# Fused attention and two expert layers: plain fp32 second tiles, halved opening transfers, and a second expert layer whose first gather precedes the search

## The chip, the cores and the metric

The kernel runs on one core of a Trainium2 chip, so nothing is exchanged with other cores. The metric is the device time of one execution in microseconds, the median of several runs. The engines are named as the profile does: PE is TensorE (PEld its weight loads), DVE VectorE, ACT ScalarE, POOL GpSimd, SP the queue engine that issues most DMAs; POOL issues the gathers and scatters by index.

## The reference, cut to what matters

```python
x = attn(q, k, v)            # 4 x 8 heads, 576 positions, head size 64, block-causal -> x: 2304 x 512
# stage 0: top-1 of 8 experts with a capacity of 576
logits = x @ w_gate; e = argmax(logits); gate = softmax(logits)[e]
keep = rank of the token among those of its expert < capacity
out = gate * (relu(x @ w1[e]) @ w2[e]) if keep else 0
# stage 1: on the result, for tokens with x @ w_skip > 0, without a capacity
y = gate2 * (relu(x @ w1b[e2]) @ w2b[e2])
out = x + y                  # the other tokens pass through
```

w1 is 512 x 1024 and w2 1024 x 512 for each expert, all fp32.

## The kernel before, in words

Attention runs over 32 heads. Its loop executes the table TURN once per head, and a hook after each entry issues side work: weights of stage 0's first expert into the eight tiles raw[0], zeros into the output (both through load_more, one 512 KB transfer per head), and steps of the routing generators.

A stage then works through tiles of 128 tokens, grouped by expert. The rows of a tile are gathered from X in HBM into XN by an indirect DMA of POOL, transposed on PE, and copied by ACT: as plain fp32 into x32, or as a high and a low part into xt. There are two ways to multiply. raw_products takes the fp32 weights as they landed (ph is the first layer, 32 products of 128 columns; py the second, 8 of 512 columns; the trace has two records for each fp32 product). products takes weights that were split into a high part (ACT) and a low part (a subtraction on DVE or POOL) in W, needs x and h split and transposed as well, and uses 24 + 24 products of 512 columns. A first tile of an expert can be raw while the weights are split beside it.

After a tile, prev scales py into Yx, scatters it to the output by the indices pidx and, in stage 0, routes those rows for stage 1 (transposes, logits, pick) and scatters Yx to X. put then enters the picked rows into the second router's table. Each is a generator whose steps are placed between the matmuls.

first(s, ...) opens a stage. Its order is written by hand in the strings of AHEAD: entry n + 1 lists what follows group n of the 24 groups of matmuls of the tile. S is one of the 16 half-tile splits, C a step of the chain (in the first tile of stage 0 the last routing of attention's output; of stage 1 the last put and prev of stage 0; in the second tile the table that orders the experts, and the gather of the third tile), A a step of prev, G the search for the first rows and the second expert with its gather, K the copy of XN and the gather of the second tile's rows, X and Y the transposes of the next rows, L a load of the second expert's weights, T the turn-over (pidx, XP). Tile one is written by at, tile two by at2 (inside a branch taken when the first expert has two full tiles, as it has here). Later tiles come from body. lo names the engine of each split's subtraction.

Engines run in order, each through its own queue; a value that steers a branch or a DMA is loaded into every engine's registers (TENSOR_LOAD) at the head of each block. SP issues in order; the reload of raw[0] for later users is queued there.

## Time and profile before

| | |
|---|---|
| median of 3 runs | 796.57 us (796.44 to 803.91) |
| the profiled execution | 797.4 us, of which the span is 795.5 us |
| mean granted clock of PE | 0.959 |
| busy: PE, DVE, ACT, POOL | 695.7, 444.3, 365.6, 322.1 us |
| attention | 0 to 247.8 us |
| stage 0, first tile at | 247.8 us; second 273.2; third 289.7 |
| stage 1, first tile at | 562.2 us; second 578.8; third 594.0 |

The span runs from the first to the last instruction; a stage begins where its first product does. Busy time of PE is modelled and overlaps at the edges, so starts of successive groups say more than durations.

### The profile page before, as it was taken

How to read it: one execution, taken by the hardware profiler on the slowest of the kernel's cores; microseconds unless marked ns; L12 is line 12 of the kernel's file. 1: busy time of each engine (PE TensorE's matmuls, PEld its weight loads, DVE VectorE, ACT ScalarE, POOL GpSimd, SP SyncE). 2: the span in 40 equal slices, each digit the busy share in tenths (PEclk: the TensorE clock that was granted, in tenths of full speed). 3: DMA queues.
4: the chain of work that ended last, by engine and by line, in shares of the span. 5: the costliest groups of instructions: out<-in, count | busy, mean ns of one | idle time of the engine just before them, and what ended most of it. 6: DMA issues, size and time to landing. Idle time of an engine off the chain costs nothing. (4 is left out here: it accounts for less than half of the span.)

```text
span 795.5 us, 14329 instructions
## 1 busy us (share of the span) xinstructions
PE 695.7 (87%) x4288; PEld 522.6 (66%) x4288; DVE 444.3 (56%) x1389; ACT 365.6 (46%) x886; POOL 322.1 (40%) x362
## 2 busy tenths in 40 slices
PE   5999989989988769987899999994889989999991
PEld 4878767768766447765567776672667667777860
DVE  5877897798875623421263435443532767632473
ACT  4877656757755123311353324432412565522371
POOL 5766555556505412211242223322533446341362
PEclk9999999999999789998999999997799999999996
DMA  8799959849312675425771111111639488110000
GB/s 169 149 220 205 227 143 194 209 81 152 69 46 57 225 260 172 134 74 194 248 258 42 60 44 44 42 64 58 222 130 367 146 282 298 37 54 16 32 25 14
DMA packets 107000, 108.61 MB, mean 137 GB/s; under 512 B 66599, under 2 KB 75815, under 8 KB 106832
## 3 DMA queue, kind: packets, MB, share of 16 engines
q1 hardware_dynamic: 100192, 87.62, 41.0%
q0 software_dynamic: 6640, 19.07, 7.2%
q8 instruction: 67, 1.10, 0.6%
q14 instruction: 101, 0.83, 0.3%
HBM read 102.81 MB, written 22.30 MB: 157 GB/s over the span
## 5 line engine op out<-in xcount | busy, mean ns | idle before, releaser
L867 PE MATMUL ph<-W,xt 128*128 128x512 f32 x456 | 127.3, 417 | 2.2 <-ACTq L1149 0.8
L843 PE MATMUL ph<-x,raw 128*128 128x128 f32 x832 | 105.6, 286 | 21.5 <-issue 9.0
L876 PE MATMUL py<-W,hT 128*128 128x512 f32 x456 | 120.4, 403 | 1.5 <-DVE hT L738 1.5
L843 PEld LDWEIGHTS ph<-x,raw 128*128 128x128 f32 x832 | 100.8, 200 | 29.9 <-issue 12.7
L714 DVE TENSOR_TENSOR W<-raw,W 128x512 fp32r<-128x512 f32 x107 | 100.4, 974 | 22.6 <-ACT W L712 19.6
L867 PEld LDWEIGHTS ph<-W,xt 128*128 128x128 f32 x456 | 81.8, 191 | 24.5 <-issue 5.5
L850 PE MATMUL py<-raw,h 128*128 128x512 f32 x208 | 96.7, 606 | 0.0
L712 ACT CAST W<-raw 128x512 fp32r<-128x512 f32 x160 | 87.6, 617 | 15.3 <-DVE full L963 6.5
L876 PEld LDWEIGHTS py<-W,hT 128*128 128x128 f32 x456 | 82.0, 189 | 18.9 <-DVE hT L738 2.2
L206 ACT ACTIVATE P<-s,nm 128x576 f32<-128x576 f32 (+4 forms) x160 | 82.7, 524 | 18.1 <-DVE nm L199 13.9
L719 POOL DMA_INDIRECT XN<-X,nidx x30 | 33.8, 1126 | 140.0 <-DVE ohv1b L503 75.2
L714 POOL TENSOR_TENSOR W<-raw,W 128x512 fp32r<-128x512 f32 x53 | 71.6, 1362 | 40.5 <-ACT W L712 40.1
L199 DVE TENSOR_REDUCE nm<-s 128x1 f32<-128x576 f32 (+4 forms) x160 | 75.3, 487 | 4.5 <-DVE s L197 0.2
L31 PE MATMUL pt<-ident,P 128*128 128x128 f32 x480 | 74.4, 283 | 1.6 <-DVE xr L1253 0.9
L187 PE MATMUL s<-KT,QT 128*128 128x320 f32 (+1 forms) x192 | 64.5, 348 | 4.9 <-ACT P L206 4.8
L106 ACT COPY PT<-pt 128x448 f32<-128x448 f32 (+2 forms) x96 | 47.2, 492 | 41.4 <-PE pt L31 41.2
L738 DVE TENSOR_TENSOR hT<-t,hT 128x512 fp32r<-128x512 f32 x38 | 26.3, 692 | 69.4 <-ACT hT L737 69.2
L31 PEld LDWEIGHTS pt<-ident,P 128*128 128x128 f32 x480 | 51.9, 142 | 17.7 <-DVE s L197 5.5
L890 ACT ACTIVATE h<-ph 128x512 f32<-128x512 f32 x38 | 22.7, 598 | 86.1 <-PE ph L867 86.1
L850 PEld LDWEIGHTS py<-raw,h 128*128 128x128 f32 x208 | 37.8, 195 | 36.1 <-issue 36.1
L188 PE MATMUL s<-KS,QT 128*128 128x320 f32 (+1 forms) x192 | 55.7, 314 | 4.6 <-DMA KS<-KT 4.6
L262 PE MATMUL o<-PT,vs 128*64 128x256 f32 (+3 forms) x448 | 56.4, 368 | 0.5 <-ACT xT L106 0.5
(256 smaller groups left out, 1037.5 us busy)
## 6 DMA issues: line engine op xcount, KB each, us to landing
raw<-in_moe_w_dram SPq DMA_DIRECT2D x152, 512.0 KB
KS<-KT SPq DMA_DIRECT2D x64, 144.0 KB
ks<-in_k_dram SPq DMA_DIRECT2D x32, 144.0 KB
qs<-in_q_dram SPq DMA_DIRECT2D x32, 144.0 KB
out_dram<-XN SPq DMA_DIRECT2D x9, 512.0 KB
vs<-in_v_dram SPq DMA_DIRECT2D x32, 128.0 KB
X<-xr SPq DMA_DIRECT2D x16, 256.0 KB
v<-in_v_dram SPq DMA_DIRECT2D x16, 32.0 KB
```

Source lines behind the costliest of these rows:

```text
L31: nc.tensor.transpose(out, in_, ident)
L187: nc.tensor.matmul(out=out, lhsT=lhs, rhs=kT[:, a:e], start=True, stop=False)
L188: nc.tensor.matmul(out=out, lhsT=lhs, rhs=kS[:, a:e].bitcast(F32R), start=False, stop=True)
L199: self.nc.vector.reduce_max(out=nm[:m], in_=self.sv[h, i], axis=AX.X, negate=True)
L206: self.nc.scalar.activation(P[:m, PO[i]:PO[i] + KN[i]], self.sv.pop((h, i)), AF.Exp, bias=self.nm.pop((h, i))[:m], accum_out=sm[:m, i:i + 1],)
L262: nc.tensor.matmul(out=ps[64 * j:64 * j + 64, a - q0:q1 - q0], lhsT=vs[:, j, c, :] if c < 4 else self.v4[p % 3][:, j], rhs=PT[:, KO[c] + a ...
L712: nc.scalar.copy(hi, src)
L714: eng.tensor_tensor(out=lo, in0=src, in1=hi.bitcast(F32), op=ALU.subtract)
L843: nc.tensor.matmul(out=ph[j // 4][:, 128 * (j % 4):128 * (j % 4) + 128], lhsT=raw[c][:, 128 * j:128 * j + 128], rhs=self.x32[:, 128 * c:12 ...
L850: nc.tensor.matmul(out=self.py, lhsT=self.h32[c // 4][:, 128 * (c % 4):128 * (c % 4) + 128], rhs=raw[4 + c // 2][:, 512 * (c % 2):512 * (c ...
L867: nc.tensor.matmul(out=ps, lhsT=xt[p][:, 128 * c:128 * c + 128], rhs=W[w][c][:, 512 * half:512 * half + 512], start=n == 0, stop=n == 11,)
L876: nc.tensor.matmul(out=ps, lhsT=self.hT[c // 4][p][:, 128 * (c % 4):128 * (c % 4) + 128], rhs=W[w][4 + c // 2][:, 512 * (c % 2):512 * (c % ...
```

## The change

The second tile of each stage is computed by raw_products, so its rows are only copied to x32, and the weights need to be split by the third tile. All 16 subtractions go to DVE; six (stage 0) or eight (stage 1) splits lie in the first tile and the rest in the second. The first tile's result has buffers of its own, Y0 and pidx0. raw[0] is reloaded after the second tile. In stage 1, G stops at the gather, the search for the second expert (H) comes behind the products of the first layer, and most steps of the chain come after the first products. In stage 0 the routing chain is no longer interleaved with splits. In attention, the weights and zeros go out in transfers of 256 KB, up to two per head, over heads 9 to 29 in place of one of 512 KB per head over heads 4 to 20. h serves both kinds of tile (h32 is gone).

```diff
-    def prev(self, s):
-        nc = self.nc
+    def prev(self, s, first=False):
+        nc = self.nc
+        Yx, pidx = (self.Y0, self.pidx0) if first else (self.Yx, self.pidx)
         gate = self.XP[:, DM:DM + 1]
         if s == 0:
-            nc.scalar.activation(self.Yx[:, 0:DM], self.py, AF.Copy, scale=gate)
+            nc.scalar.activation(Yx[:, 0:DM], self.py, AF.Copy, scale=gate)
         else:
             nc.vector.scalar_tensor_tensor(
-                out=self.Yx[:, 0:DM], in0=self.py, scalar=gate, in1=self.XP[:, 0:DM], op0=ALU.mult, op1=ALU.add
+                out=Yx[:, 0:DM], in0=self.py, scalar=gate, in1=self.XP[:, 0:DM], op0=ALU.mult, op1=ALU.add
             )
         yield
-        self.indirect(self.out, self.Yx[:, 0:DM], self.pidx, scatter=True)
+        self.indirect(self.out, Yx[:, 0:DM], pidx, scatter=True)
         if s:
             return
-        ps = self.t4(self.Yx)
+        ps = self.t4(Yx)
         nc.scalar.copy(self.yT, ps)
         yield
...
         yield from self.r2.pick(
-            self.lg, self.valid, self.pval, self.Yx[:, DM:DM + 1],
-            lambda: self.indirect(self.X, self.Yx, self.pidx, scatter=True),
+            self.lg, self.valid, self.pval, Yx[:, DM:DM + 1],
+            lambda: self.indirect(self.X, Yx, pidx, scatter=True),
         )
...
-                        out=self.py, lhsT=self.h32[c // 4][:, 128 * (c % 4):128 * (c % 4) + 128],
+                        out=self.py, lhsT=self.h[c // 4][:, 128 * (c % 4):128 * (c % 4) + 128],
                         rhs=raw[4 + c // 2][:, 512 * (c % 2):512 * (c % 2) + 512], start=c == 0, stop=c == 7,
                     )
             if n in (5, 11):
-                nc.scalar.activation(self.h32[n // 6], ph[n // 6], AF.Relu)
+                nc.scalar.activation(self.h[n // 6], ph[n // 6], AF.Relu)
             at(n)
...
     def first(self, s, router, chain, after=None, cap=None):
         nc, tc = self.nc, self.tc
         plan = self.AHEAD[s]
+
         split = self.split(s, self.raw[0], plan["lo"])
+        done = plan["at"].count("S")
+        ahead = self.ahead(s, router)
...
-            self.reload(s, 0, range(8))
+            if not two:
+                self.reload(s, 0, range(8))
             router.index(self.idx[s], router.T, "i")
...
             elif t == "G":
-                for _ in self.ahead(s, router):
+                for _ in range(3):
+                    next(ahead)
+            elif t == "H":
+                for _ in ahead:
                     pass
             elif t == "Y":
                 self.next_x("r")
             elif t == "X":
-                self.next_x("x")
+                self.next_x("r")
...
             elif t == "K":
                 self.keep(s, self.XC, self.XN)
                 self.gather(s, self.XN, self.pre[:, 1:2], self.rows)
             elif t == "T":
-                self.turn_over(s, lambda: nc.vector.tensor_copy(self.pidx, self.pre[:, 0:1]))
-
-        script(plan["at"], one, True)
-        for x in split, chain, load:
+                self.turn_over(s, self.pidx0, lambda: nc.vector.tensor_copy(self.pidx0, self.pre[:, 0:1]))
+
+        script(plan["at"], one)
+        for x in chain, load:
...
         with tc.If(flag(2) > 0) as two:
-            steps, prev = experts(True), self.prev(s)
+            steps, prev, rest = experts(True), self.prev(s, True), self.split(s, self.raw[0], plan["lo"], done)
 
             def act(t):
                 if t == "A":
                     next(prev, None)
+                elif t == "S":
+                    next(rest, None)
...
@@ -1076,13 +1086,19 @@
                 elif t == "T":
                     for _ in prev:
                         pass
-                    self.turn_over(s, lambda: nc.vector.tensor_copy(self.pidx, self.pre[:, 1:2]))
+                    self.turn_over(s, self.pidx, lambda: nc.vector.tensor_copy(self.pidx, self.pre[:, 1:2]))
 
             script(plan["at2"], act)
+            for _ in rest:
+                pass
+            self.reload(s, 0, range(8))
         with two.Else():
+            for _ in self.split(s, self.raw[0], plan["lo"], done):
+                pass
             for _ in experts(False):
                 pass
             self.next_x("xr")
+            nc.vector.tensor_copy(self.pidx, self.pidx0)
         self.count = {k: self.value(0, k) for k in range(2)}
         self.base, self.number = {0: 0}, {}
         self.base[1] = self.value(3, 1, mybir.EngineType.DVE)
@@ -1090,14 +1106,14 @@
 
     AHEAD = (
         dict(
-            lo="VPPVPPVPPPPPPPVV",
-            at="KSSSCCCCCCCCCC SS S S S CCSCC CSSC S S S S S S CCC CC CC C CLLL LLL LL C C CX C CT",
-            at2="KCCCCC C CC - AAA CAC CA AAC A CC - - - - AAAC - - A - - X - - - T",
+            lo="VVVVVVVVVVVVVVVV",
+            at="KCCCCCCCCCC - - - - CCCC CCCCCCCC CCC - S - S S S - S - LLLS LLL LLC - - X - T",
+            at2="KACCCCC CC CA C CA C CA CAS AS AS AS AS S S S S S - - X - - - - T",
         ),
         dict(
-            lo="PVPVVPVPPPPVVPPP",
-            at="GSCCCCCSSCSCCSCSCYKCCCCS SSC CSC - - SS - CCCCS LCCS CSLCC L LCL C LSLL - - X - - C - - - - T",
-            at2="KAACCCCCCCC - C C - - - CCCCC - - - - - - - - - - - - X - - - T",
+            lo="VVVVVVVVVVVVVVVV",
+            at="GCCCCYK CC CC - C CC C CCCCCCC H - - - CL CL LLS LLS LLS S S S S X S - T",
+            at2="KACCCCC CCA C C CS CS CS S S S S S S - - - - - - X - - - - T",
         ),
     )
...
+        def weights(i):
+            m, h = i // 2, i % 2
+            t, w1, w2 = raw[0][m][:, 512 * h:512 * h + 512], w11, w12
+            if m < 4:
+                nc.sync.dma_start(out=t, in_=w1[0, 128 * m:128 * m + 128, 512 * h:512 * h + 512])
+            else:
+                r = 256 * (m - 4) + 128 * h
+                nc.sync.dma_start(out=t, in_=w2[0, r:r + 128, :])
+
+        def zeros(i):
+            nc.sync.dma_start(out=out[128 * i:128 * i + 128, :], in_=M.XN[:, 0:DM])
+
+        def capacity_value():
+            nc.vector.tensor_copy(capf[:, 0:1], capi[:, 0:1].bitcast(U32))
...
+        def load_more(h, part):
+            n = 2 * h + part
+            if n == 6:
                 load_small()
-            elif step < 8:
-                m = step
-                w1, w2 = w11, w12
-                t = raw[0][m]
...
+            i = n - 18
+            if 0 <= i < 42 and i % 5 != 4:
+                i -= i // 5
+                if i % 2 == 0 and i < 32:
+                    weights(i // 2)
                 else:
...
+                    zeros(i // 2 if i < 32 else i - 16)
 
...
@@ -1335,8 +1357,8 @@
         step, n = [0], len(A.TURN)
 
         def hook():
-            if step[0] % n == 0:
-                load_more(step[0] // n - 10)
+            if step[0] % n in (0, n // 2):
+                load_more(step[0] // n - 6, int(step[0] % n > 0))
             if step[0] % n in A.SIDE:
```

Three places show how the order moves. DVE in the first tile of stage 0, from the rank to the first ORa (rra and ranka are ranks, OJa and ORa the operands of the permute matmuls that TensorE waits for, W the low parts), before:

```order
L429 TENSOR_REDUCE ranka<-rra 128x5
L432 TENSOR_TENSOR gea<-j_80,ranka 128x95
L714 TENSOR_TENSOR W_3844<-raw_179,W_3836 128x512 x2
L435 SCALAR_TENSOR_TENSOR kva<-ranka,cap,vb 128x5
L438 TENSOR_TENSOR Ja<-gea 128x90
L440 TENSOR_REDUCE rma<-gea 128x5
L443 TENSOR_TENSOR ohva<-oha,kva 128x40
L444 SCALAR_TENSOR_TENSOR rma<-rma,ranka 128x5
L449 TENSOR_TENSOR OJa<-ohva,Ja 128x144
L455 TENSOR_SCALAR ORa<-iotam,rma 128x128
```

and after, from the rank on:

```order
L429 TENSOR_REDUCE ranka<-rra 128x5
L432 TENSOR_TENSOR gea<-j_80,ranka 128x95
L435 SCALAR_TENSOR_TENSOR kva<-ranka,cap,vb 128x5
L438 TENSOR_TENSOR Ja<-gea 128x90
L440 TENSOR_REDUCE rma<-gea 128x5
L443 TENSOR_TENSOR ohva<-oha,kva 128x40
L444 SCALAR_TENSOR_TENSOR rma<-rma,ranka 128x5
L449 TENSOR_TENSOR OJa<-ohva,Ja 128x144
L455 TENSOR_SCALAR ORa<-iotam,rma 128x128
L449 TENSOR_TENSOR OJa<-ohva,Ja 128x144
L455 TENSOR_SCALAR ORa<-iotam,rma 128x128
```

The two subtractions between gea and kva are gone; six subtractions now stand behind the fifth ORa, ahead of the sum into Ta.

PE at the end of the first tile of stage 0 and the start of the second (pt is the permute), before:

```order
L850 MATMUL py<-raw_177,h_3863 128x512 x2
L850 MATMUL py<-raw_178,h_3864 128x512
L462 MATMUL pt<-OJa,ORa 128x144 x5
L850 MATMUL py<-raw_178,h_3864 128x512
L31 MATMUL t<-ident,XN 128x128 x4
L850 MATMUL py<-raw_179,h_3864 128x512 x2
L988 TENSOR_LOAD flags
L1062 COMPARE_AND_BRANCH
L867 MATMUL ph<-W_3829,xt_196 128x512
L867 MATMUL ph<-W_3830,xt_196 128x512
L867 MATMUL ph<-W_3831,xt_196 128x512
```

and after, with the start of the second tile and the place of the first result's transposes:

```order
L462 MATMUL pt<-OJa,ORa 128x144 x5
L854 MATMUL py<-raw_178,h_3875 128x512 x2
L31 MATMUL t<-ident,XN 128x128 x4
L854 MATMUL py<-raw_179,h_3875 128x512 x2
L995 TENSOR_LOAD flags
L1070 COMPARE_AND_BRANCH
L847 MATMUL ph<-x_198,raw_172 128x128
L847 MATMUL ph<-x_198,raw_173 128x128
L847 MATMUL ph<-x_198,raw_174 128x128
L847 MATMUL ph<-x_198,raw_175 128x128
L847 MATMUL ph<-x_198,raw_172 128x128
L31 MATMUL t<-ident,Y_3881 128x128 x4
```

The permute stands one product earlier, and the second tile begins with raw products, with the transposes of Y0 (here Y_3881) after five of them.

PE at the opening of stage 1 (oh1b, OJb and ORb belong to put, lgT to prev, XN holds the gathered rows), before:

```order
L508 MATMUL g<-oh1b,ONE 128x8
L31 MATMUL t<-ident,Yx 128x128 x4
L765 MATMUL g<-yT,w_171 32x128 x4
L31 MATMUL g<-ident,lgT 128x128
L541 MATMUL g<-OJb,ORb 128x144
L31 MATMUL t<-ident,XN 128x128 x4
L507 LDWEIGHTS LT
L507 MATMUL g<-oh1b,LT 128x16
L508 LDWEIGHTS ONE
L508 MATMUL g<-oh1b,ONE 128x8
L843 MATMUL ph<-x_198,raw_172 128x128
L843 MATMUL ph<-x_198,raw_173 128x128
```

and after:

```order
L508 MATMUL g<-oh1b,ONE 128x8
L31 MATMUL t<-ident,Yx 128x128 x4
L769 MATMUL g<-yT,w_171 32x128 x4
L31 MATMUL g<-ident,lgT 128x128
L31 MATMUL t<-ident,XN 128x128 x4
L847 MATMUL ph<-x_198,raw_172 128x128
L847 MATMUL ph<-x_198,raw_173 128x128
L847 MATMUL ph<-x_198,raw_174 128x128
```

The put matmuls on ORb and the second pair on oh1b no longer stand ahead of the first raw product.

## Rows read from the trace of the kernel before

**Rows 1.** Windows by stage (from:to, length, busy us per engine with instructions, clock, DMA share, GB/s).
```profile
247.80:311.70 63.90, 50.19 (x247) 35.74 (x246) 33.61 (x113) 19.81 (x40) 22.63 (x23) 0.87 0.57 193
...
543.00:594.80 51.80, 34.44 (x170) 25.92 (x171) 22.62 (x89) 15.73 (x30) 22.55 (x21) 0.80 0.40 139
```

**Rows 2.** Timeline of PE, first tile of stage 0 (start, us, instruction, [idle <-releaser]).
```profile
252.07 0.20 PE L408 MATMUL pt<-oha,LT 128*128 128x48 bf16 x1 [1.23 <-DVE oha L398]
...
256.56 4.46 PE L850 MATMUL py<-raw,h 128*128 128x512 f32 x10
266.08 2.06 PE L462 MATMUL pt<-OJa,ORa 128*128 128x144 f32 x5 [5.06 <-DVE ORa L455]
...
273.22 2.53 PE L867 MATMUL ph<-W,xt 128*128 128x512 f32 x8
```

**Rows 3.** Timeline of DVE in the same tile, and one row of POOL.
```profile
250.12 1.04 DVE L380 TENSOR_TENSOR eva<-lg,mxa 128x40 f32<-128x40 f32 x1
...
253.64 0.84 DVE L714 TENSOR_TENSOR W<-raw,W 128x512 fp32r<-128x512 f32 x1 [0.87 <-ACT W L712]
...
258.21 0.20 DVE L429 TENSOR_REDUCE ranka<-rra 128x5 f32<-128x40 f32 x1
...
259.40 3.48 DVE L714 TENSOR_TENSOR W<-raw,W 128x512 fp32r<-128x512 f32 x2
...
264.27 1.12 DVE L443 TENSOR_TENSOR ohva<-oha,kva 128x40 f32<-128x40 bf16 x1
...
267.31 0.28 DVE L455 TENSOR_SCALAR ORa<-iotam,rma 128x128 fp32r<-128x128 f32 x1
...
252.64 12.70 POOL L714 TENSOR_TENSOR W<-raw,W 128x512 fp32r<-128x512 f32 x9 [1.54 <-ACT W L712]
```

**Rows 4.** Timeline of all engines between the second and third tile of stage 0.
```profile
289.67 0.73 PE L867 MATMUL ph<-W,xt 128*128 128x512 f32 x2 [0.78 <-ACTq L1149]
292.41 0.15 DVE L1079 COPY pidx<-pre 128x1 int32<-128x1 int32 x1 [3.55 <-DMA X<-Yx,pidx]
...
296.13 1.08 PE L31 MATMUL t<-ident,Yx 128*128 128x128 f32 x4 [5.73 <-DVEq L1149]
```

**Rows 5.** Timeline of PE: two tiles of stage 0, then a raw tile of stage 1.
```profile
311.69 0.63 PE L867 MATMUL ph<-W,xt 128*128 128x512 f32 x2
...
326.26 0.63 PE L867 MATMUL ph<-W,xt 128*128 128x512 f32 x2
...
654.69 7.38 PE L843 MATMUL ph<-x,raw 128*128 128x128 f32 x64 [0.90 <-ACT W L712]
...
668.82 4.53 PE L867 MATMUL ph<-W,xt 128*128 128x512 f32 x16
```

**Rows 6.** Timelines of DVE, POOL and PE at the opening of stage 1.
```profile
548.08 0.21 DVE L963 TENSOR_SCALAR full<-cntb 128x1 f32<-128x1 f32 x2 [5.11 <-DVEq L1143]
...
550.21 1.07 POOL L719 DMA_INDIRECT XN<-X,pre  x1 [11.86 <-DVE actb L559]
...
553.45 0.17 PE L507 MATMUL g<-oh1b,LT 128*128 128x16 bf16 x1 [10.48 <-DVE oh1b L501]
...
560.17 0.46 PE L541 MATMUL g<-OJb,ORb 128*128 128x144 f32 x1 [3.30 <-DVE ORb L538]
...
562.22 6.54 PE L843 MATMUL ph<-x,raw 128*128 128x128 f32 x36 [0.52 <-ACT x L741]
...
578.75 4.31 PE L867 MATMUL ph<-W,xt 128*128 128x512 f32 x16
```

**Rows 7.** Timeline of PE, start of the third tile of stage 1.
```profile
594.04 1.17 PE L867 MATMUL ph<-W,xt 128*128 128x512 f32 x4 [0.70 <-PEq L1149]
```

**Rows 8.** Window of the second tile of stage 0.
```profile
273.20:289.70 16.50, 14.81 (x76) 10.79 (x74) 7.78 (x34) 4.99 (x10) 3.51 (x5) 0.99 0.40 127
```

**Rows 9.** DMA issues: the gathers by pre (count, median us to landing).
```profile
XN<-X,pre POOLq DMA_INDIRECT x4, 3.5
```

**Rows 10.** Waits of PE in attention (us in total, times, longest).
```profile
PE s L188 <- DMA KS<-KT: 4.6, 5, 1.7
```

More of the change, by code (lines that the diff above doesn't have):

```diff
@@ L650, in open @@
         self.hT = [[st.tile([128, 512], F32R, name=f"hT{i}{p}") for p in range(2)] for i in range(2)]
-        self.h32 = [st.tile([128, 512], F32, name=f"h32{i}") for i in range(2)]
         self.Yx = st.tile([128, DM + 1], F32, name="Yx")
+        self.Y0 = st.tile([128, DM + 1], F32, name="Y0")
+        self.pidx0 = st.tile([128, 1], I32, name="pidx0")
         self.yT = st.tile([128, DM], F32, name="yT")
@@ L660, in open @@
         nc.gpsimd.memset(self.Yx, 0.0)
+        nc.gpsimd.memset(self.Y0, 0.0)
     def more(self):
@@ L700, with split @@
     )
-    def split(self, s, raw, lows=None):
+    def split(self, s, raw, lows=None, start=0):
         nc = self.nc
         lows = lows or self.PLAN[s]["lo"]
-        for n, i in enumerate(self.ORDER):
+        for n, i in list(enumerate(self.ORDER))[start:]:
             k, o = i // 2, 512 * (i % 2)
@@ L822, in keep, with turn_over @@
         )
-    def turn_over(self, s, rows):
+    def turn_over(self, s, pidx, rows):
         nc = self.nc
@@ L829, in turn_over @@
         if s == 0:
-            nc.vector.tensor_scalar_add(self.pval, self.pidx, 1.0)
+            nc.vector.tensor_scalar_add(self.pval, pidx, 1.0)
             nc.vector.tensor_scalar(
@@ L913, in at @@
                         pass
-                self.turn_over(s, lambda: self.column(self.idx[s], self.pidx, self.base[k] + j))
+                self.turn_over(s, self.pidx, lambda: self.column(self.idx[s], self.pidx, self.base[k] + j))
             if n == turn[2]:
@@ L1015, in experts, with script @@
             self.later, self.number = self.value(0, 3, sp), {3: self.value(4, 3, sp)}
-            self.reload(s, 0, range(8))
+            if not two:
+                self.reload(s, 0, range(8))
             router.index(self.idx[s], router.T, "i")
             yield
-        def script(text, act, raw=False):
+        def script(text, act):
             text = text.split()
@@ L1027, in at @@
                     act(t)
-            if raw:
-                self.raw_products(self.raw[0], at)
-            else:
-                self.products(s, at)
+            self.raw_products(self.raw[0], at)
         load = loads()
@@ L1211, in load_small @@
             nc.sync.dma_start(out=w9[:, :, NE], in_=wskip.rearrange("(c p) -> p c", p=128))
-        def load_more(step):
-            if step < -1:
-                return
-            if step == -1:
-                load_small()
-            elif step < 8:
-                m = step
-                w1, w2 = w11, w12
-                t = raw[0][m]
-                if m < 4:
-                    nc.sync.dma_start(out=t, in_=w1[0, 128 * m:128 * m + 128, :])
-                else:
-                    nc.sync.dma_start(
-                        out=t.rearrange("p (c d) -> p c d", c=2),
-                        in_=w2[0, 256 * (m - 4):256 * (m - 4) + 256, :].rearrange("(c p) d -> p c d", p=128),
-                    )
-            elif step < 17:
-                m, n = step - 8, NTOK // 9
-                nc.sync.dma_start(
-                    out=out[n * m:n * m + n, :].rearrange("(c p) d -> p c d", p=128),
-                    in_=M.XN[:, 0:DM].unsqueeze(1).to_broadcast([128, n // 128, DM]),
-                )
-                if m == 0:
-                    nc.vector.tensor_copy(capf[:, 0:1], capi[:, 0:1].bitcast(U32))
-                    nc.vector.tensor_copy(capf[:, 1:2], capi[:, 1:2])
-                    nc.vector.scalar_tensor_tensor(
-                        out=cap, in0=capf[:, 1:2], scalar=4294967296.0, in1=capf[:, 0:1], op0=ALU.mult, op1=ALU.add
-                    )
@@ new lines, in weights @@
+        def weights(i):
[10 more added lines that the diff above has]
+            nc.vector.tensor_copy(capf[:, 0:1], capi[:, 0:1].bitcast(U32))
+            nc.vector.tensor_copy(capf[:, 1:2], capi[:, 1:2])
+            nc.vector.scalar_tensor_tensor(
+                out=cap, in0=capf[:, 1:2], scalar=4294967296.0, in1=capf[:, 0:1], op0=ALU.mult, op1=ALU.add
+            )
@@ L1243, in pair @@
+        def load_more(h, part):
+            n = 2 * h + part
+            if n == 6:
+                load_small()
+            elif n == 17:
+                capacity_value()
+            i = n - 18
[3 more added lines that the diff above has]
+                    weights(i // 2)
+                else:
+                    zeros(i // 2 if i < 32 else i - 16)
         def pair(b, hp):
```

## Prediction

> **What bounds the kernel now.** I read the windows by stage first. The openings of the two feed-forward stages are where TensorE is least busy: 50.2 of 63.9 us in the first and 34.4 of 51.8 us in the second, at granted clocks of 0.87 and 0.80 [rows 1]. The reader is to see 31 us of idle TensorE in 116 us, and its clock lowered by it. The timelines of the openings then tell which wait ends last.
>
> Stage 0: TensorE stops after ten records of the second layer and waits 5.06 us at the permute matmuls for VectorE's ORa [rows 2]. VectorE's routing chain is late because of the splits: seven of its small operations took 1.04 to 1.25 us (the first and the last are shown) where such an operation takes 0.20, while GpSimd ran nine split subtractions in a row; and three split subtractions stand in the chain itself, of 0.84 and twice 1.74 us, one with a wait of 0.87 ahead of it [rows 3]. After the second tile TensorE waits 0.78 and then 5.73 us. VectorE's copy to pidx was held 3.55 us, until 292.41, by the scatter X<-Yx that still read pidx, and TensorE's transposes of Yx were released by VectorE's branch 3.72 us after that copy began [rows 4].
>
> Stage 1: VectorE wakes at 548.08 and the gather is issued at 550.21, but TensorE's first matmul comes at 553.45 (behind the search for the second expert on VectorE). Then it waits 3.30 us for ORb, with the transposes of the gathered rows queued behind that, and the first raw product starts at 562.22 [rows 6].
>
> **The sum** is made against the profiled execution, 797.4 us (span 795.5 and 1.9 around it); the median of the three runs is 796.57, 0.8 us lower.
>
> **First tile of stage 0.** The chain from 250.12 to the end of the last ORa at 267.59 is 17.5 us [rows 3]. Out of it go the splits and the wait between them (3.48 + 0.84 + 0.87 = 5.2) and the slowed operations' excess (7 x 1.1 - 7 x 0.2 = 6.3). That leaves 6.0, so ORa is ready at 256. TensorE also lost 1.23 us at oha [rows 2]; 0.84 of that is the excess of the one slowed operation ahead of oha, and a split that stood ahead of the chain is gone too, so I take the whole. Its second layer then starts at 256.56 - 1.23 = 255.3 and reaches the permute after eight records, near 259, three microseconds after ORa: the 5.06 go. Sixteen records at 4.46 / 10 = 0.446 us are 7.1, the permute at full clock about half of its 2.06, the transposes of XN half of the 1.08 that four took at the low clock [rows 4]. The second tile starts near 264.0 instead of 273.22: **-9.2 us**. Bounds: -5 (only the wait goes) to -10.
>
> **Second tile of stage 0.** It becomes raw. Before: 273.22 to 289.67 less 0.78 is 15.7 us. A raw tile of stage 1, which has no routing, took 668.82 - 654.69 = 14.1 [rows 5]. A split tile took 14.6 in stage 0 (326.26 - 311.69) [rows 5] and as much, 593.34 - 578.75 = 14.6, in the second tile of stage 1 [rows 6, 7], so routing adds 0 to 2 us: 14.1 to 16.1, I take 15.7, **0**.
>
> Ten of the sixteen splits lie in this tile, their subtractions all on VectorE. GpSimd has none left, so I price one at 0.84, the row nearest to a subtraction alone: 8.4 us, beside what VectorE does in that tile anyway, 7.78 [rows 8], less two subtractions for h of about 0.7. That is 14.8 under 15.7 us of TensorE, and VectorE begins it while TensorE still ends the first tile: covered, but barely.
>
> A rule that speaks against this part: raw products are plain fp32. The Trainium skill, "FP8 and Floating Point Precision", section TensorE Precision Notes, says that true FP32 takes four passes through the array. By it, as an estimate, 8,192 columns four times are 32,768, against 48 products of 512 columns, 24,576: 3.4 us more for each of the two tiles at full clock, and the sum would be 780. Rows 5 to 7 do not show it between whole tiles, since a split tile also transposes h and waits for hT; they decide.
>
> **Between second and third tile.** The first tile now scatters from Y0 by pidx0, so nothing holds the copy to pidx. Without its 3.55 us VectorE's branch would have released TensorE at 292.6 instead of 296.13. TensorE would have been there at 289.67 + 0.73 = 290.4, and the transposes of the next rows now have four fp32 products behind them (eight records, 3.6 us) instead of eight split ones (8 x 14.6 / 48 = 2.4), which covers 1.2 more. Left: 292.6 - 290.4 - 1.2 = 1.0 us, or 2 where VectorE's subtractions run over. So VectorE's branch is still late next, by little. The third tile took 311.69 - 289.67 = 22.0 us, the next one 14.6 [rows 4, 5]. The excess of 7.4 (the wait, and products at the low clock behind it) becomes about 1.4: **-6.0 us** (-3 to -7).
>
> **Stage 1.** The search moves behind the first tile's products, and so do most put steps and all splits. VectorE's index is ready as before and the gather is still issued at 550.2. The four chain steps that stay ahead of the products fill TensorE from 553.45 to 556.87 (560.17 less the wait) [rows 6]; without the search ahead of them they start some 4 us earlier and end before the gather does. A gather lands 3.5 us after its issue [rows 9]: 553.7. From the put matmul at 560.17 to the first product at 562.22 the transposes and the copy to x32 took 2.05, some 0.3 of it the put's, so 1.7: products from 555.4, **-6.8 us** (-4 to -7.5). The first tile keeps its 16.5 us, with two rounds of small put matmuls inside instead of one: **+0.4**. The second tile was 14.6 and a raw one is 14.1: **-0.3**. The second expert's loads now wait for flags that come some 7 us later relative to the products; the first expert's further tiles lie between, which hides it; without them it would cost those 7.
>
> **Attention.** The 17 transfers of 512 KB become 34 of 256 KB over more heads. TensorE's waits for KS are 4.6 us in five places [rows 10]. Bounds 0 to -4.6, and +2 if new waits arise in the later heads. I take **-2**, since fewer bytes per head compete but more heads have them. The memset of Y0 on GpSimd stands ahead of the second gather, whose rows are wanted a tile later: nothing. The slot-0 reload moves behind the second tile, on SP with nothing but later loads queued behind it; that tile now ends before 280, and the expert it loads comes after two others: nothing, unless it came out tens of microseconds late.
>
> Sum: -9.2 + 0 - 6.0 - 6.8 + 0.4 - 0.3 - 2 = -23.9, so 797.4 - 23.9 = **773.5 us**.
>
> **Rivals.**
> 1. VectorE becomes the bound of stage 0's second tile: its ten subtractions take the 1.74 us of the slowed rows [rows 3], 9 us more than counted, nearly all of it uncovered: 782.5. For it: the cover is under 3 us. Against: GpSimd is left with a few keeps and gathers.
> 2. One part gives little: the gather of stage 1 lands later and saves half, and attention gains nothing: +5.4, 778 to 780.
> 3. Slower: the spread transfers hold up the KS copies in attention. There are 34 places with a transfer instead of 17. If each made TensorE wait 0.70 us the gain of 23.9 is gone; from 0.94 us each the kernel is 1% slower, 805. For it: the waits seen average 0.92 us and the longest is 1.7 [rows 10]. Against: they are five in the whole stage, and each copy has half as many bytes ahead of it.
> 4. Better: all KS waits go and the third tile starts without a wait: 769 or less.
>
> The Trainium skill speaks for the third: "DMA: Bandwidth & Descriptors", section Measured, advises transfers of 1 MiB and more. By it the halved transfers cost the queues time and the sum loses its -2 and turns to a loss in attention; the trace of before has no transfer of 256 KB to HBM by which to judge it, and the chance below is the one I give that mechanism.
>
> **How the numbers follow.** Forecast 0.60 (its own spread 768 to 778), first rival 0.13, second 0.13, fourth 0.05, slower 0.04; 0.05 is left for shortfalls that end within 1% of before. One per cent, 8 us, is about what a measurement of this kernel can tell from no change. The range is to hold 0.8: from 766 to 785 it takes in the bounds and the first two rivals and leaves out the rest. Faster by over 1%: 0.60 + 0.13 + 0.13 + 0.05 = 0.91; within 1%: 0.05; slower: 0.04.
>
> **What would show it.** Right: no wait for ORa before the permute, and the clock near 1.0 through stage 0's opening; the second tile about 9 us earlier; VectorE's copy to pidx not held by a scatter, and at most 2 us of wait at the third tile; stage 1's first raw product 7 us after VectorE's first operation instead of 14; KS waits below 3 us. Wrong: VectorE's subtractions above 1 us in the second tile and TensorE waiting for its branch or for W; a gather that lands 5 us or more after its issue; KS waits in more places than five; later experts waiting for weights, which I price at nothing.

## The result and the profile after

The changed kernel takes 775.41 us (774.74 to 780.13, 4 runs) against 796.51 for the kernel before, a ratio of 0.972 (95% interval 0.966 to 0.978). In a second group of runs, beside other kernels, it took 773.86 against 794.15, 0.975 (0.972 to 0.979). The forecast was 773.5, with 766 to 785 as its range. The profiled execution has a span of 774.3 us, 21.2 less than before, at a mean granted clock of 0.970 instead of 0.959.

The windows of the changed kernel, one for each of the first three tiles of stage 0 and of stage 1 (columns as in [rows 1]):

```profile
251.66:266.91 15.25, 15.25 (x98) 11.36 (x97) 13.07 (x57) 5.10 (x10) 0.19 (x1) 1.00 0.72 217
266.91:283.25 16.34, 15.71 (x98) 11.20 (x97) 10.66 (x34) 9.37 (x19) 6.84 (x5) 1.00 0.81 288
283.25:298.33 15.08, 14.32 (x76) 10.74 (x77) 5.54 (x29) 4.72 (x10) 3.51 (x5) 1.00 0.76 259
541.33:558.58 17.25, 17.25 (x89) 13.37 (x90) 10.02 (x40) 6.52 (x14) 3.40 (x4) 0.86 0.34 115
558.58:574.29 15.71, 14.83 (x85) 10.33 (x84) 11.40 (x32) 5.94 (x12) 4.02 (x4) 1.00 0.78 277
574.29:586.95 12.66, 12.66 (x61) 10.11 (x62) 3.05 (x7) 3.45 (x6) 3.38 (x4) 1.00 1.02 376
```

Through stage 0's opening TensorE is busy all the time in the first tile and its clock stays at 1.00; the opening of [rows 1] ran at 0.87. The timeline of PE there, against [rows 2, 4, 5]:

```profile
251.66 3.07 PE L847 MATMUL ph<-x,raw 128*128 128x128 f32 x26
...
262.07 1.08 PE L462 MATMUL pt<-OJa,ORa 128*128 128x144 f32 x5
...
266.91 1.28 PE L847 MATMUL ph<-x,raw 128*128 128x128 f32 x10
...
283.25 0.70 PE L871 MATMUL ph<-W,xt 128*128 128x512 f32 x2 [0.63 <-PEq L1165]
284.71 0.63 PE L31 MATMUL t<-ident,Yx 128*128 128x128 f32 x4 [0.75 <-DVEq L1165]
...
298.33 0.63 PE L871 MATMUL ph<-W,xt 128*128 128x512 f32 x2
```

The permute no longer waits for ORa, and the 5.73 us ahead of the transposes of Yx are 0.75. VectorE's side of it, against [rows 3]:

```profile
253.27 0.20 DVE L380 TENSOR_TENSOR eva<-lg,mxa 128x40 f32<-128x40 f32 x1
...
258.41 0.28 DVE L455 TENSOR_SCALAR ORa<-iotam,rma 128x128 fp32r<-128x128 f32 x1
258.60 1.29 DVE L717 TENSOR_TENSOR W<-raw,W 128x512 fp32r<-128x512 f32 x2
...
276.38 3.69 DVE L717 TENSOR_TENSOR W<-raw,W 128x512 fp32r<-128x512 f32 x6
```

From eva to the last ORa the chain takes 5.4 us where it took 17.5, and a subtraction of two in a row 0.65. At the opening of stage 1 (PE, with one row each of DVE and POOL), against [rows 6]:

```profile
534.24 0.21 DVE L967 TENSOR_SCALAR full<-cntb 128x1 f32<-128x1 f32 x2 [5.89 <-DVEq L1159]
...
535.24 0.17 PE L507 MATMUL g<-oh1b,LT 128*128 128x16 bf16 x1 [6.89 <-DVE oh1b L501]
...
536.01 1.08 POOL L722 DMA_INDIRECT XN<-X,pre  x1 [12.27 <-DVE rrb L517]
...
539.48 1.11 PE L31 MATMUL t<-ident,XN 128*128 128x128 f32 x4 [0.82 <-DMA XN<-X,pre]
541.33 4.64 PE L847 MATMUL ph<-x,raw 128*128 128x128 f32 x20 [0.73 <-ACT x L744]
```

The first product now comes 7.09 us behind VectorE's first operation (14.14 before), and the wait that decides is the gather's, with ScalarE's copy of the transposed rows (0.73) behind it. Attention is the part that went against the forecast: stage 0's first product moved from 247.78 to 251.66. Its timeline shows three waits for KS, the copy of a head's KT that a DMA of SP makes and that the scores s are computed from:

```profile
82.29 0.39 PE L188 MATMUL s<-KS,QT 128*128 128x320 f32 x1 [1.15 <-DMA KS<-KT]
...
131.55 0.63 PE L188 MATMUL s<-KS,QT 128*128 128x320 f32 x1 [3.65 <-DMA KS<-KT]
...
193.78 0.38 PE L188 MATMUL s<-KS,QT 128*128 128x320 f32 x1 [2.15 <-DMA KS<-KT]
```

and the windows show the low clock at the second of them (0.50, that is 1.2 GHz, the lower of its two levels, from 131 to 136, right behind the idle 3.65 us):

```profile
130.00:140.00 10.00, 8.45 (x52) 7.12 (x53) 4.25 (x12) 3.04 (x9) 2.32 (x3) 0.67 1.16 205
140.00:150.00 10.00, 10.00 (x96) 7.75 (x94) 7.21 (x21) 8.17 (x27) 7.32 (x7) 1.00 0.64 179
```

The first tile of stage 1 also still runs at a low clock: 0.86, as in the kernel before, with 0.50 from 541 to 545. TensorE was busy for 7.75 of the 17.33 us ahead of that tile.

Each piece of the two profiled executions, from one start of a tile to the next:

| piece | before | after | difference | predicted |
|---|---|---|---|---|
| attention | 247.78 | 251.66 | +3.88 | -2 |
| stage 0, first tile | 25.44 | 15.25 | -10.19 | -9.2 |
| second tile, with the wait behind it | 16.45 | 16.34 | -0.11 | 0 |
| third tile | 22.02 | 15.08 | -6.94 | -6.0 |
| further tiles, to VectorE's first operation of stage 1 | 236.39 | 235.91 | -0.48 | |
| from there to the first product | 14.14 | 7.09 | -7.05 | -6.8 |
| first tile | 16.53 | 17.25 | +0.72 | +0.4 |
| second tile | 15.29 | 15.71 | +0.42 | -0.3 |
| third tile | 13.65 | 12.66 | -0.99 | |
| the rest | 187.81 | 187.35 | -0.46 | |
| span | 795.5 | 774.3 | -21.2 | -23.9 |

### The profile page after: what moved, and what is told of

The parts are those of the page before. It is cut to its first block, busy times and chain, and to the rows that moved or that the text cites. A ratio compares the mean times of both kernels' runs of the same rounds, so it can differ in the third digit from the quotient of the medians.

```text
span 774.3 us, 14404 instructions
## 1 busy us (share of the span) xinstructions
PE 695.2 (90%) x4336; PEld 523.3 (68%) x4336; DVE 443.1 (57%) x1404; ACT 363.4 (47%) x882; POOL 299.1 (39%) x342
## 5 line engine op out<-in xcount | busy, mean ns | idle before, releaser
L847 PE MATMUL ph<-x,raw 128*128 128x128 f32 x960 | 121.1, 285 | 16.3 <-issue 6.4
L847 PEld LDWEIGHTS ph<-x,raw 128*128 128x128 f32 x960 | 115.9, 199 | 26.3 <-issue 11.7
L717 DVE TENSOR_TENSOR W<-raw,W 128x512 fp32r<-128x512 f32 x128 | 113.2, 931 | 23.3 <-ACT W L715 22.9
L871 PE MATMUL ph<-W,xt 128*128 128x512 f32 x408 | 112.3, 412 | 1.6 <-PEq L1165 1.3
L854 PE MATMUL py<-raw,h 128*128 128x512 f32 x240 | 108.8, 594 | 0.0
L880 PE MATMUL py<-W,hT 128*128 128x512 f32 x408 | 107.2, 403 | 0.0
L871 PEld LDWEIGHTS ph<-W,xt 128*128 128x128 f32 x408 | 72.2, 189 | 20.9 <-issue 6.8
L880 PEld LDWEIGHTS py<-W,hT 128*128 128x128 f32 x408 | 73.5, 189 | 14.8
L854 PEld LDWEIGHTS py<-raw,h 128*128 128x128 f32 x240 | 42.8, 190 | 41.3 <-issue 41.1
L717 POOL TENSOR_TENSOR W<-raw,W 128x512 fp32r<-128x512 f32 x32 | 44.3, 1383 | 34.1 <-ACT W L715 33.8
```

The costliest lines, as they stand in the source:

```text
L717: eng.tensor_tensor(out=lo, in0=src, in1=hi.bitcast(F32), op=ALU.subtract)
L847: nc.tensor.matmul(out=ph[j // 4][:, 128 * (j % 4):128 * (j % 4) + 128], lhsT=raw[c][:, 128 * j:128 * j + 128], rhs=self.x32[:, 128 * c:12 ...
L854: nc.tensor.matmul(out=self.py, lhsT=self.h[c // 4][:, 128 * (c % 4):128 * (c % 4) + 128], rhs=raw[4 + c // 2][:, 512 * (c % 2):512 * (c % ...
L871: nc.tensor.matmul(out=ps, lhsT=xt[p][:, 128 * c:128 * c + 128], rhs=W[w][c][:, 512 * half:512 * half + 512], start=n == 0, stop=n == 11,)
L880: nc.tensor.matmul(out=ps, lhsT=self.hT[c // 4][p][:, 128 * (c % 4):128 * (c % 4) + 128], rhs=W[w][4 + c // 2][:, 512 * (c % 2):512 * (c % ...
```

## Experiments

Times of different groups of runs differ by some microseconds (the kernel before took 794.15 in one and 799.85 in another on the same chip), so each run is set against the kernel before in its own group, and small edits are judged by their piece of the trace.

**Transfers in attention.** First the changed kernel with load_more as in the kernel before, and its hook:

```diff
-            if step[0] % n in (0, n // 2):
-                load_more(step[0] // n - 6, int(step[0] % n > 0))
+            if step[0] % n == 0:
+                load_more(step[0] // n - 10)
```

> The changed kernel with the opening transfers of before (17 of 512 KB, heads 4 to 20). Theory: the spread transfers are why stage 0's first product moved from 247.78 to 251.66 us: two waits for KS of 3.65 and 2.15 us, each with a lower granted clock behind it. Then the first product comes at 247.8 again, the three KS waits of 6.9 us are five of 4.6 again, and 771.5 us is the time (775.4 less 3.9). Rival: the 3.9 us come from elsewhere, or the weights that land in larger pieces make stage 0's opening wait: first product at 251 to 252, or the gain lost by stage 0's second tile, and 775 us.

Measured: 775.06 against 796.67 (0.9735, 0.970 to 0.977), a ratio that cannot be told from the changed kernel's. Stage 0's first product came at 249.43, with five KS waits of 6.2 us. That is between the two expectations, so the changed kernel ran again, beside the kernel before with the new transfers alone and two other places for them.

> The changed kernel once more, beside the next three on one chip. Theory: its attention has three waits for KS near 82, 131 and 193 us of which the second exceeds 3 us and costs the granted clock behind it; stage 0's first product comes at 250 to 253 us, and the time is 775 to 778. Rival: those waits were an accident of one execution, attention ends at 247 to 249 as before, and the time is below 773.

Measured: 773.86 against 794.15, and attention ended at 246.34, with KS waits of 4.3 us, the longest 2.8, and no low clock behind them (1.00 in the window from 130 to 140). The same attention code put the first product at 246.34, 246.46, 247.34, 248.19, 251.66, 253.06 and 253.58 in seven profiled executions. The wait near 131 us goes with it: it was 3.41, 3.65 and 4.62 us in the three that came last, with a clock of 0.66 to 0.67 in the window from 130 to 140, and 2.26 to 3.04 in the other four, with 0.83 to 1.00. Why it is long in some executions no run shows.

> The kernel before with the spread transfers alone (256 KB halves over heads 9 to 29). Theory: they cost attention 2.5 to 4 us: stage 0's first product at 250.5 to 252 instead of 247.8, 799 to 801 against 796.5. Rival, as the prediction had it: they give 2 us, 794.5. No difference within 1 us would say that the 3.9 us of the first comparison are scatter between executions.

Measured: 795.48 against 794.15, ratio 1.0015 (0.9989 to 1.004), that is between -0.9 and +3.2 us; first product at 247.50. So the new transfers account for 1.3 of the +3.88 of the first comparison by the middle value, 3.2 at most, and the rest is scatter between executions; a gain of 2 us lies outside the interval. Then the first of the two other places:

```diff
-            if step[0] % n in (0, n // 2):
-                load_more(step[0] // n - 6, int(step[0] % n > 0))
+            if step[0] % n in (21, 22):
+                load_more(step[0] // n - 6, step[0] % n - 21)
```

> The changed kernel with both halves of a head issued right behind that head's KS copies instead of ahead of them (17 table entries and 4 entries ahead). Theory: the first of two KS pairs that SP issues together has no transfer ahead, the second two; the wait near 131 us falls from 3.65 to about 2 and the clock drop behind it goes: 2 to 3 us less than the changed kernel. Rival: KS is late because SP was held earlier by the store of xr, and its place among the transfers does not matter: no change.

Measured: 772.61 against 794.15, 0.9717 (0.969 to 0.975), 1.2 us under the changed kernel and inside the scatter; KS waits 2.7 us in three places, first product at 246.29. The second place, with load_more keeping only its other duties:

```diff
+            h, at = step[0] // n - 6, step[0] % n
+            if h % 2 == 1 and h >= 5 and at in (22, 23, 24):
+                transfer(3 * (h - 5) // 2 + at - 22)
```

> The changed kernel with the halves issued three at a time in every odd head from 5 to 27, behind the second of the two KS pairs that SP issues together, so that no transfer stands between SP's release and a KS copy. Theory: the waits for KS fall below 3 us in total and no clock drop is left in attention; stage 0's first product at 246 to 248, 3 to 5 us less than the changed kernel, 771 to 772. Rival: the loads of the next heads that now stand behind three transfers come late and TensorE waits for ks or rawK instead; no gain.

Measured: **769.49** (768.43 to 771.93) against 794.15, 0.9691 (0.966 to 0.972), the best of all, 4.4 us under the changed kernel of the same group, whose runs scatter more (770.80 to 777.76). The first product came at 242.87, and KS waits were 1.4 us in two places; a second kernel with these transfers, the last run below, had it at 243.07 with 1.7 us. The transfers also go out in threes here and begin four heads earlier, which no run separates from their place. SP's timeline in the changed kernel:

```profile
108.89 0.55 SPq L136 DMA_DIRECT2D KS<-KT  x1
114.96 0.47 SPq L1282 DMA_DIRECT2D X<-xr  x1
...
125.20 0.50 SPq L1234 DMA_DIRECT2D raw<-in_moe_w_dram  x1
...
127.00 0.59 SPq L1240 DMA_DIRECT2D out_dram<-XN  x1
127.63 0.46 SPq L1234 DMA_DIRECT2D raw<-in_moe_w_dram  x1
128.20 0.47 SPq L135 DMA_DIRECT2D KS<-KT  x1
```

and with the transfers behind both KS pairs:

```profile
114.75 0.47 SPq L1282 DMA_DIRECT2D X<-xr  x1
...
125.46 0.54 SPq L135 DMA_DIRECT2D KS<-KT  x1
126.09 0.55 SPq L136 DMA_DIRECT2D KS<-KT  x1
126.69 0.59 SPq L1237 DMA_DIRECT2D raw<-in_moe_w_dram  x1
```

SP issues nothing from 109.4 to 115, since a store of xr waits for VectorE; then it works off what has queued up, at about 0.6 us for each. The second pair of KS copies of that burst goes out 13.2 us behind the release in the first case (128.20 - 114.96) and 10.7 in the second (125.46 - 114.75). The three transfers ahead of it in the first case, at 125.20, 127.00 and 127.63, hold the queue for 0.60, 0.63 and 0.57 us, 1.8 of the difference of 2.5.

**Own buffers for the first tile's result**: the kernel before with Y0 and pidx0 (prev, turn_over and their callers as in the change, and one pair of h for both kinds of tile):

```diff
-            steps, prev = experts(True), self.prev(s)
+            steps, prev = experts(True), self.prev(s, True)
...
-                self.turn_over(s, lambda: nc.vector.tensor_copy(self.pidx, self.pre[:, 0:1]))
+                self.turn_over(s, self.pidx0, lambda: nc.vector.tensor_copy(self.pidx0, self.pre[:, 0:1]))
```

> The kernel before with one part alone: the first tile's result gets buffers of its own (Y0, pidx0, and one pair of h for both kinds of tile to make room). Theory: VectorE's copy to pidx is no longer held by the scatter for 3.55 us; the waits of 0.78 and 5.73 us ahead of stage 0's third tile become 3 or less, and with the low clock behind them 4 to 5.5 us go: 791 to 792.5 us. Rival: the branch with its register loads is as late without the scatter, and the wait stays above 5 us: 796 us.

Measured: 790.89 against 796.67, 0.9932 (0.991 to 0.996). PE behind the second tile:

```profile
288.57 0.74 PE L870 MATMUL ph<-W,xt 128*128 128x512 f32 x2 [0.73 <-ACTq L1153]
291.43 0.63 PE L31 MATMUL t<-ident,Yx 128*128 128x128 f32 x4 [2.13 <-DVEq L1153]
...
306.56 0.63 PE L870 MATMUL ph<-W,xt 128*128 128x512 f32 x2
```

The wait of 5.73 is 2.13, and the third tile takes 306.56 - 288.57 = 17.99 instead of 22.02: 4.0 of the 6.94 us are the buffers' alone. VectorE's branch comes next, as forecast; its 2.13 fall to 0.75 behind raw products.

**What slows the routing chain in stage 0.** oha is the one-hot choice of experts, which the rank matmuls need. Two runs put the six splits of the first tile ahead of the chain in the changed kernel, first with the subtractions on GpSimd, then on VectorE (lo unchanged):

```diff
-            lo="VVVVVVVVVVVVVVVV",
-            at="KCCCCCCCCCC - - - - CCCC CCCCCCCC CCC - S - S S S - S - LLLS LLL LLC - - X - T",
+            lo="PPPPPPVVVVVVVVVV",
+            at="KSSSSSSCCCCCCCCCC - - - - CCCC CCCCCCCC CCC - - - - - - - - - LLL LLL LLC - - X - T",
```

> The changed kernel with the six splits of stage 0's first tile put ahead of the routing chain and their subtractions given to GpSimd: the chain on VectorE holds no split, but GpSimd subtracts beside it. Theory: GpSimd's subtractions slow VectorE's small operations to 1.0 to 1.25 us, as in the kernel before; the last ORa comes 5 to 6 us later, TensorE waits 2 to 4 us at the permute, and the first tile takes 17 to 19 us instead of 15.25: 777 to 779 us. Rival: only the splits that stood inside VectorE's own queue were slow; then small operations stay at 0.15 to 0.3 us, the tile at 15.3 and the time at 775.

Measured: 784.90 against 796.67 (0.9867, 0.982 to 0.991). The timeline, rows of POOL, DVE and PE:

```profile
247.60 7.45 POOL L717 TENSOR_TENSOR W<-raw,W 128x512 fp32r<-128x512 f32 x6 [0.71 <-ACT W L715]
...
248.97 1.22 DVE L380 TENSOR_TENSOR eva<-lg,mxa 128x40 f32<-128x40 f32 x1
...
252.67 0.20 DVE L390 TENSOR_REDUCE mna<-eva 128x5 f32<-128x40 f32 x1
...
254.03 1.05 DVE L401 TENSOR_SCALAR sea<-sea 128x5 f32<-128x5 f32 x1
...
254.05 0.20 PE L408 MATMUL pt<-oha,LT 128*128 128x48 bf16 x1 [3.65 <-DVE oha L398]
...
268.04 1.28 PE L847 MATMUL ph<-x,raw 128*128 128x128 f32 x10
```

Five small operations took 0.95 to 1.30 us while GpSimd subtracted (1.24 us each), the reductions between them 0.20. The tile took 268.04 - 247.34 = 20.7 us, above the 17 to 19 expected: the wait is at oha and not at the permute, and behind it the last 38 records (19 products) of the first layer took 6.12 us instead of 4.49, at a lower clock (0.92 over the tile).

> The changed kernel with the six splits of stage 0's first tile put ahead of the routing chain as in the run with GpSimd beside the chain, but subtracted on VectorE. Theory: this has the price of the queue alone, without GpSimd: six subtractions of 0.65 us and their waits for ScalarE's casts stand ahead of the chain, 3.9 to 5 us, the small operations stay at 0.15 to 0.3 us; the first tile takes 16.5 to 18.5 instead of 15.25 us, and less than the 20.7 of the run with GpSimd: 777 to 778 us. Rival: the delay lies in the place in VectorE's queue and not in GpSimd, and this costs as much as that run, 20 us or more.

Measured: 780.28 against 797.01 (0.9774, 0.972 to 0.983). VectorE and PE:

```profile
248.40 3.70 DVE L717 TENSOR_TENSOR W<-raw,W 128x512 fp32r<-128x512 f32 x6 [2.15 <-ACT W L715]
...
253.53 0.20 DVE L380 TENSOR_TENSOR eva<-lg,mxa 128x40 f32<-128x40 f32 x1
...
254.64 0.20 PE L408 MATMUL pt<-oha,LT 128*128 128x48 bf16 x1 [3.38 <-DVE oha L398]
...
268.62 1.28 PE L847 MATMUL ph<-x,raw 128*128 128x128 f32 x10
```

The small operations stay at 0.20, and yet the tile takes 268.62 - 248.19 = 20.4 us. The theory was wrong on the size (16.5 to 18.5): six subtractions in VectorE's own queue delay oha nearly as much as GpSimd's beside it (3.38 against 3.65), and here too the 38 records behind that wait took 6.12 us. The rival, place in the queue, is as dear. Both runs put the splits ahead of the chain; neither has them inside it, as the kernel before.

**Stage 1: search and put ahead of the products.** Three runs, by the string alone (H the search; six more C the first put; the third both):

```diff
-            at="GCCCCYK CC CC - C CC C CCCCCCC H - - - CL ...
+            at="GHCCCCYK CC CC - C CC C CCCCCCC - - - - CL ...
+            at="GCCCCCCCCCCYK - - - - C C CCCCCCC H - - - CL ...
+            at="GHCCCCCCCCCCYK - - - - C C CCCCCCC - - - - CL ...
```

> The changed kernel with stage 1's search for the second expert (16 small operations of VectorE, 2.4 us) put back ahead of the first products, behind the gather's issue; the put steps stay behind the products. Theory: the gather lands 3.5 us after its issue and hides a part; TensorE's first matmul comes 2.4 us later and the first product 1.6 us later, 8.7 us behind VectorE's first operation instead of 7.1: 777 us. Rival one: the gather hides it all, 7.1 to 7.4 and 775.5. Rival two: the search was the whole of the 7.05 us gained, 14 and 782.

Measured: 780.43 against 796.67 (0.9795, 0.975 to 0.984; its attention ended at 253.06). First product 544.86 - 536.20 = 8.66 us behind VectorE's first operation, as expected to a tenth.

> The changed kernel with six more steps of stage 1's chain (the first put up to its matmuls on ORb, the rest of prev) back ahead of the first products; the search stays behind them. Theory: TensorE waits about 3.3 us for ORb again, with the transposes of the gathered rows queued behind; the first product comes 10.5 to 12.5 us behind VectorE's first operation instead of 7.1: 778.5 to 780. With the 1.6 us of the run with the search ahead this makes up the 7.05 us of the change. Rival: the gather's landing hides the put, the first product comes at 7.1 to 8, and it was the search and the order of the two together that cost the time.

Measured: 774.34 against 797.01 (0.9715, 0.967 to 0.976); 541.12 - 532.96 = 8.16. TensorE waited 1.69 for ORb, not 3.3: the theory failed, and the rival's 7.1 to 8 held but for 0.2.

> The changed kernel with both the search and the first put ahead of stage 1's first products, as in the kernel before, but with no split among them. The two alone cost 1.57 and 1.07 us, far from 7.05. Theory: each alone hides partly under the gather's landing and the two follow each other on VectorE, and the splits that stood among them made up the rest (a small operation of 1.98 us beside a subtraction on GpSimd, and two subtractions of 0.67 ahead of ORb): the first product comes 10.5 to 11 us behind VectorE's first operation, against 7.09 and 14.14, so that the splits are worth 3 to 3.6: 777 to 778 us. Rival one: the two do not add, 8.7 to 9, and the splits were worth over 5. Rival two: 13 to 14, the splits cost nothing.

Measured: 781.30 against 799.85 (0.9759, 0.972 to 0.980; attention ended at 253.58). Rows of DVE, then PE:

```profile
537.03 0.21 DVE L967 TENSOR_SCALAR full<-cntb 128x1 f32<-128x1 f32 x2 [6.12 <-DVEq L1159]
...
545.81 0.46 PE L541 MATMUL g<-OJb,ORb 128*128 128x144 f32 x1 [1.69 <-DVE ORb L538]
...
547.86 5.79 PE L847 MATMUL ph<-x,raw 128*128 128x128 f32 x32 [0.73 <-ACT x L744]
```

547.86 - 537.03 = 10.83. So 3.74 of the 7.05 us are search and put, more than 1.57 + 1.07 since the gather's landing hides a part of either alone, and 3.31, by difference, the splits that stood among them. Two places in the kernel before make up 3.0 of it: a small operation that took 1.98 us beside a subtraction on GpSimd (0.35 in the third run), and two subtractions of 0.67 and 0.68 ahead of ORb:

```profile
550.63 1.98 DVE L563 TENSOR_SCALAR actb<-pinb 1x8 f32<-1x8 f32 x1
```

A later opening gives some of its cost back in the first tile, which took 17.25 us at a clock of 0.86 in the changed kernel and 16.48, 16.64 and 16.76 at 0.90, 0.88 and 0.88 in the three runs.

**A split second tile in stage 1.** On the best version; at2 loses its S, and the second tile goes through products:

```diff
-            at="GCCCCYK CC CC - C CC C CCCCCCC H - - - CL CL LLS LLS LLS S S S S X S - T",
+            at="GCCCCYK CC CC S CS CCS CS CCCCCCC H SS S S CLS CLS LLS LLS LLS S S S - X - - T",
```

> The kernel of the run before (transfers behind both KS copies) with stage 1's second tile split again: all 16 splits lie in the first tile, eight of them moved there, and the second tile multiplies by the parts. Rows of the changed kernel: its raw second tile took 15.08 us, the split tile behind it 12.66. Theory: the raw tile is dearer by the difference, the eight splits more find room beside the first tile (17.25 us, VectorE 10 us busy), and the second tile takes 12.7 to 13.5: 1.5 to 2.4 us less than the run before, 767 to 768. Rival: the splits crowd VectorE and ScalarE in the first tile, the chain or the parts come late, and the second tile waits: no gain or a loss, 769.5 to 772.

Measured: 773.21 against 797.01, 0.970 (0.967 to 0.973), no gain over 0.9691. PE in that tile:

```profile
553.37 1.49 PE L871 MATMUL ph<-W,xt 128*128 128x512 f32 x4
557.55 4.62 PE L871 MATMUL ph<-W,xt 128*128 128x512 f32 x12 [2.69 <-DVE pidx L1065]
...
571.63 4.25 PE L871 MATMUL ph<-W,xt 128*128 128x512 f32 x16 [0.63 <-PEq L1168]
```

Twelve subtractions ran on VectorE from 548.96 to 556.89 ahead of the low part of x, so TensorE waited 2.69 (the row names the copy to pidx, which stands right behind that part), and the tile took 571.63 - 0.63 - 553.37 = 17.6 us against 15.5 of the raw one (552.98 to 568.48 in the best version). Twelve of its products also ran at a low clock behind that wait (4.62 us; twelve took 3.06 at a clock of 1.00 in the kernel before). In this order the raw tile is worth its dearer products because it needs no parts yet; an order with the low part of x ahead of the subtractions was not run.

## Why the prediction was right

The sum of -23.9 and the measured -21.2 are as close as they are partly by luck: attention came out 5.9 us worse than forecast in that execution, and everything else together 3.2 us better (-25.1 against -21.9). The waits that were to go in the two openings did go.

**First tile of stage 0** (-9.2, measured -10.19). The waits for oha and ORa are gone as the working had it, and the clock stays up. The two prices in it, 5.2 for splits and 6.3 for slowed operations, were read as two costs; the runs do not separate them in the old order, and show that six splits ahead of the chain, on either engine, cost 5.2 to 5.5 us of the tile (20.4 and 20.7 against 15.25). The working overlooked a fourth subtraction in the chain, 0.69 us at 252.08, which brings its 6.0 for the chain to 5.3, against 5.4 measured. Most of the last microsecond is a size: the sixteen records of the second layer took 6.5 us (3.03, 1.76 and 1.72 between starts), not 7.1.

**Second tile** (0, measured -0.11; without the waits behind it 15.7 in both). VectorE's ten subtractions cost 0.62 to 0.69 each, not 0.84, and are covered; the first rival, VectorE as the bound, did not come.

**Third tile** (-6.0, measured -6.94). The scatter's hold on pidx was the larger part (4.0), shown by the buffers alone; the rest is 2.13 - 0.75 of VectorE's branch and the low clock behind it (the tile's clock was 0.84 before, 0.91 with the buffers alone and 1.00 after the change).

**Opening of stage 1** (-6.8, measured -7.05). The forecast held, with the gather's landing as the wait that decides: TensorE takes up its rows 3.47 us behind the issue (539.48 - 536.01). The shares are 3.74 and 3.31 as above.

**First and second tile of stage 1** (+0.4 and -0.3, measured +0.72 and +0.42). The second has the sign wrong, and the term that was mis-sized is the raw tile: priced 14.1, it took 15.71 - 0.63 = 15.08, against 15.29 - 0.70 = 14.59 before. The row behind the 14.1 was a tile with no branch behind it, and such a tile still takes 14.13 after the change:

```profile
662.49 7.38 PE L847 MATMUL ph<-x,raw 128*128 128x128 f32 x64 [1.07 <-ACT W L715]
...
676.62 4.30 PE L871 MATMUL ph<-W,xt 128*128 128x512 f32 x16
```

In the second tile the last eight records run out ahead of the branch (3.60 us to their end, 3.04 to the next tile's start in the other), and 0.25 us is a wait for the gathered rows. That rule of the Trainium skill which spoke against this part ("FP8 and Floating Point Precision", TensorE Precision Notes) has its sign right: by four passes the estimate was 3.4 us, and the trace has 1.5 between whole tiles with no branch behind them (14.13 against the 12.66 of the split third tile). Of the gap, 0.8 us are the split tile's two transposes of h (0.39 each, at 578.10 and 581.37); the rest stays open. The loss does not appear in the sum, as the split tile had to wait when it was tried.

**Attention** (-2, measured +3.88 in that execution, +1.3 with -0.9 to +3.2 for the part alone). This step failed, and with it the sign of KS waits below 3 us (6.9 in three places): fewer bytes ahead of a KS copy did not help, since three transfers stood ahead of the second of two pairs of copies that SP issues in one burst, and the two longest waits fell in windows with a lower clock (0.67 and 0.83). The third rival names the right place, but prices it by 34 waits; there were three. The rule of the page "DMA: Bandwidth & Descriptors" of the Trainium skill (section Measured, transfers of 1 MiB and more) finds no price here for halves of 256 KB that the measurement can tell from zero; another place and grouping of them in SP's queue is worth 4.4 us.

Not predicted: the third tile of stage 1, 0.99 us shorter (TensorE's wait of 0.72 for VectorE's branch is gone there), and some 0.5 us in each of the two long stretches, of which the runs show no cause.

## What to carry to other kernels

In the opening of a stage, give the engine that decides it nothing but the chain that TensorE waits for; here six subtractions ahead of the chain cost the tile as much in the engine's own queue (20.4 us) as on the engine beside it (20.7). A transfer that can go at any time belongs behind the copies that someone waits for, counted per burst of the queue and not per loop step, and a store that waits holds all that stands behind it. Price a step that moves under a landing transfer by running it with its neighbours: alone, the slack hides it.

## What had not been expected of the hardware

GpSimd's scatter of Y to X took 4.35 us where others of it took 1.0, in all eleven executions of the changed order; VectorE ran six subtractions in a row beside it, in the first profile of the changed kernel from 276.38 to 280.07. With the own buffers alone, in the old order, it took 1.02, so the buffer is not the cause; no run kept the new order and took the subtractions away:

```profile
276.63 4.35 POOL L722 DMA_INDIRECT X<-Y,pidx  x1 [4.83 <-DVE ohvb L493]
```

Beside GpSimd's subtractions four of VectorE's operations with two inputs took 0.95 to 1.30 us and its reductions 0.20. The Trainium skill, "SBUF — State Buffer", section Who interferes with whom, says that instructions with two SBUF inputs contend with GpSimd's reads and that reductions never do; the rows agree with both. A fifth operation, a TENSOR_SCALAR with one input, took 1.05. And the clock: it fell to 0.50 behind the wait for KS of 3.65 us, but also behind the one of 2.15 (from 195 to 198) and, in the run with the transfers behind each head's KS copies, behind one of 1.71 (from 142 to 145), while it stayed at 1.00 behind that of 2.78 in the second execution. Among these shorter waits the length alone did not tell; the three of 3.41 to 4.62 us all came with 0.66 to 0.67 in their window.
